# Window attention and a SiLU MLP on one core: the second chunk's maximum sent earlier by GpSimd's queue, block 2's rows shared by two engines, later blocks' steps moved

## The chip, the core and the metric

The kernel runs on one core of a Trainium2 chip. The metric is the device time of one execution in microseconds (us); the median of three runs stands for the kernel. One execution is also profiled. Engines: PE (TensorE), DVE (VectorE), ACT (ScalarE), POOL (GpSimd) and SP (SyncE, which here only issues DMAs). PEld is PE's loading of weights.

## What is computed

The input x has 4 batches of 4096 rows of 192. Each row is replaced by a weighted sum over itself and the six rows before it (zeros ahead of a batch's first), with weights from a softmax over 7 values for each of 8 heads. An MLP follows, without biases:

```python
w = softmax(weight_gen, axis=-1)                  # B, S, 8 heads, 7 taps
x_unf = the 7 rows ending at s, split by head     # zeros ahead of row 0
out = einsum('bshk,bskhg->bshg', w, x_unf)        # 16384 x 192
h = out @ w_in                                    # 192 x 2048
g = h * sigmoid(h)
result = g @ w_out                                # 2048 x 192
```

## The kernel before

A partition holds 128 consecutive rows of x (32 partitions make a batch), plus a halo of the six rows before them. The work goes in 32 blocks of `TB` = 4 rows per partition, 512 rows a block. Blocks are loaded in chunks: chunk 0 is block 0, chunk 1 block 1, chunk 2 blocks 2 and 3, and from chunk 3 on four blocks each, seven such chunks.

For a chunk, `softmax_steps` (lines 288 to 317) makes the weights: `top`, `sub`, `exp`, `tot`, `rec`, `norm`. From chunk 2 on POOL does `sub` and `norm`, ACT `exp`, DVE the rest. `scale_steps` (line 321) finds the largest absolute value of the chunk's x for a power-of-two scale: DVE reduces the rows (line 332) to one value per partition (`m_x`), which has to reach all partitions. `absmax_to_all` does that by PE, for chunk 0 and the weights; `absmax_by_dma` (line 169) writes the 128 values to DRAM (`d_x`) and reads them back to every partition (`mb_x`), both DMAs on SP's queue, and DVE reduces them (line 184).

For a block, `prep_steps` (line 386) makes seven products of x and weights (`mul`, line 396) and adds them up (`add`, line 402), on POOL for the first `share` taps and on DVE for the others; block 2 has all seven on POOL, later blocks three. `hi` on ACT and `lo` on DVE (lines 371, 374) split the result in two fp16 parts `xs`, a DMA transposes it to `xt` and two more swap its halves to `xu`. Blocks 0 and 1 (`early_prep`, line 419) have their products on DVE and the sums on PE in fp32 (line 439).

The MLP goes by pairs of 128 columns of w_in, eight pairs to a block. `mm1` (line 479) makes `h` in PSUM from `xt` and `xu`, 18 matmuls a pair; `act` on ACT makes silu and its fp16 high part `gh` (lines 487, 488); `lower` on DVE makes the low part `gl` (line 493) and with it frees the PSUM tile, of which there are four; `mm2` (lines 507, 516) adds the pair's part of the second product. `finish` (lines 535, 536) scales a block out. `mm1` runs 2 to 4 pairs ahead of `mm2` (`lead_of`): three in the first five pairs of a block, two in the last three.

The fp32 weights w_in and w_out come as integer words and are converted by DVE and ACT in the course of blocks 0 and 1: `merge` (lines 232, 233), then `move`, `shift`, `upper`, `lower` for each pair (lines 242 to 252).

Each engine works off its own list in order, so what matters is where an instruction stands in its engine's list and what it waits for. Two tables set that. `OPENING` gives, for the sixteen pairs of blocks 0 and 1, the steps emitted ahead of a pair's `mm1` and behind its `act`: `m0` to `m6` and `t0` to `t6` are block 1's products and sums, `a` and `b` the reduction of chunk 1's x and its two DMAs, `c` and `d` the reduction of what comes back and the scales, `g` the `gl` of the pair before, `I`, `O`, `i`, `o` the conversion, `x` the maximum of w_out. `START` gives for the steps of later chunks and blocks the half pair at which they are emitted: a time u is worked off behind the half pair of that number, a block has 16 of them, and the times of block b's steps (`any_p` on POOL, `any_v` on DVE) and of a chunk's (`any_s` softmax, `any_x` scale) count from two blocks ahead of it. A step of time 9 stands behind the fifth pair, pair 4; one of time 16 between the two halves of the next block's first pair.

## Time and profile before

| | us |
|---|---|
| median of 3 runs (lowest, highest) | 1115.7 (1114.89, 1116.55) |
| profiled execution, its own time | 1114.89 |
| its span, first to last instruction | 1113.1 |
| PE busy (share of the span) | 1056.1 (95%) |
| DVE, ACT, POOL busy | 800.0, 775.1, 323.6 |

Busy time by stretch of the span, in us:

| stretch | PE | DVE | ACT | POOL | granted PE clock (1 is 2.4 GHz) |
|---|---|---|---|---|---|
| 0 to 60 | 38.68 | 42.65 | 15.45 | 5.22 | 0.78 |
| 60 to 100 | 32.52 | 34.35 | 25.67 | 16.21 | 0.86 |
| 100 to 145 | 36.44 | 35.07 | 28.73 | 17.75 | 0.92 |
| 145 to 1113.1 | 948.46 | 687.97 | 705.20 | 284.45 | 1.00 |

The first three stretches are the opening: blocks 0 and 1 with the conversion of the weights. In a timeline row the brackets at the end give the idle time of the engine just before the instruction and what ended it; a row with x2 or more merges neighbours of one kind. A matmul's end is modelled, so rows of PE overlap.

### The profile page before, as it was taken

The page shows a single profiled execution, that of the slowest core. Times are in us where ns is not written, and L with a number is a line of the kernel's source. Part 1 is how long each engine was busy: PE and PEld are TensorE (multiplying, and loading weights), DVE is VectorE, ACT ScalarE, POOL GpSimd, SP SyncE. Part 2 cuts the span into 40 slices and gives each one's busy share as a digit, 9 for nine tenths or more (in the row PEclk, how much of TensorE's full clock was granted, in tenths as well). Part 3 has the DMA queues.
Part 4 walks back from the last instruction along what each step waited for, and adds up shares of the span by engine and source line. Part 5 has one row for each costly group of instructions (what it writes and reads, how often), then busy time and mean ns, then how long its engine had stood idle before and what let it go on. Part 6 is the DMA issues. An engine that isn't in the chain of part 4 may idle for free.

```text
span 1113.1 us, 37056 instructions
## 1 busy us (share of the span) xinstructions
PE 1056.1 (95%) x16592; PEld 806.7 (72%) x16592; DVE 800.0 (72%) x1158; ACT 775.1 (70%) x1245; POOL 323.6 (29%) x185
## 2 busy tenths in 40 slices
PE   6687999999999999999999999999999999999997
PEld 4344667777777777787777777777777777777776
DVE  6788788666876678666886668766886668766643
ACT  1364787776777777667877777678777768777774
POOL 1008304333252124333061233333043332521100
PEclk8778999999999999999999999999999999999999
DMA  9312104221141113311141111421041112211110
GB/s 244 115 29 98 30 29 142 45 44 31 44 141 30 31 45 93 83 40 44 31 129 42 44 45 31 141 45 37 24 141 45 45 30 45 44 34 31 44 45 16
DMA packets 71453, 68.17 MB, mean 61 GB/s; under 512 B 52607, under 2 KB 64383, under 8 KB 69886
## 3 DMA queue, kind: packets, MB, share of 16 engines
q1 hardware_dynamic: 70592, 63.34, 20.8%
q10 hardware_dynamic: 702, 2.47, 0.9%
q8 instruction: 129, 2.11, 0.8%
q14 instruction: 30, 0.25, 0.1%
HBM read 28.44 MB, written 12.59 MB: 37 GB/s over the span
## 4 chain that ended last, share of the span: by engine, by line
PE 70%; ACT 11%; DVE 10%; issue 4%; DMA 3%; POOL 1%; ACTq 0%; DVEq 0%; POOLq 0%
PE acc L507 35%; PE h L479 34%; ACT h L487 4%; DVE gl L493 3%; ACT gh L488 2%; POOL wc L314 1%; PE acc L516 1%; ACT t L535 1%; ACT L302 1%; DMA raw<-in_moe_w_in_dram 1%; ACT L487 1%; DMA d_x<-m_x 1%; ACT xs L371 1%; ACT wc L302 1%; DVE pr L396 1%
## 5 line engine op out<-in xcount | busy, mean ns | idle before, releaser
L493 DVE SCALAR_TENSOR_TENSOR gl<-h,gup,gh 128x512 f16<-128x512 f32 x512 | 380.3, 746 | 262.7 <-ACT gh L488 262.5
L507 PE MATMUL acc<-wo,gh 64*128 64x192 f16 x7616 | 527.4, 243 | 0.0
L507 PE MATMUL acc<-wo,gl 64*128 64x192 f16 x3808 | 509.6, 243 | 4.5 <-DVE gl L493 4.5
L487 ACT ACTIVATE h<-h,inv 128x512 f32<-128x512 f32 x512 | 336.3, 657 | 250.4 <-PE h L479 248.6
L507 PEld LDWEIGHTS <-gh 64*128 64x128 f16 x7616 | 450.7, 94 | 22.1
L479 PEld LDWEIGHTS <-w 64*128 64x128 f16 x4608 | 284.1, 95 | 232.1 <-issue 35.8
L488 ACT ACTIVATE gh<-h,gup 128x512 f16<-128x512 f32 x512 | 352.0, 688 | 16.7
L479 PE MATMUL h<-xt,w 64*128 64x512 f16 x2304 | 325.3, 380 | 27.2 <-DVE gl L493 17.6
L479 PE MATMUL h<-xu,w 64*128 64x512 f16 x2304 | 321.7, 380 | 0.0
L507 PEld LDWEIGHTS <-gl 64*128 64x128 f16 x3808 | 280.6, 94 | 6.1 <-DVE gl L493 6.1
L396 POOL TENSOR_TENSOR pr<-xc,wc 128x768 f32<-128x768 f32 x94 | 156.1, 1674 | 403.5 <-DVE pr L402 381.3
L402 POOL TENSOR_TENSOR pr<-pr,pr 128x768 f32<-128x768 f32 x64 | 138.1, 2157 | 5.0
L396 DVE TENSOR_TENSOR pr<-xc,wc 128x768 f32<-128x768 f32 x116 | 124.4, 1073 | 9.5 <-POOL wc L314 9.5
L402 DVE TENSOR_TENSOR pr<-pr,pr 128x768 f32<-128x768 f32 x116 | 110.0, 949 | 0.0
L298 POOL TENSOR_TENSOR wc<-wc,wm 128x896 f32<-128x896 f32 (+1 forms) x8 | 13.3, 1658 | 152.3 <-DVE wm L295 152.3
L314 POOL TENSOR_TENSOR wc<-wc,ws 128x896 f32<-128x896 f32 (+1 forms) x8 | 13.3, 1658 | 145.2 <-DVE ws L311 116.3
L536 DVE SCALAR_TENSOR_TENSOR o<-acc,od,t 128x192 f32<-128x192 f32 x120 | 41.6, 407 | 3.3 <-ACT t L535 3.3
L516 PE MATMUL acc<-wo,gh 128*128 128x192 f16 x288 | 39.4, 252 | 4.3 <-ACT wo L249 2.0
L535 ACT ACTIVATE t<-acc,od 128x192 f32<-128x192 f32 x120 | 40.7, 426 | 3.6 <-PE acc L516 3.6
L332 DVE TENSOR_REDUCE xm<-xc 128x1 f32<-128x960 f32 (+4 forms) x32 | 40.9, 1278 | 0.0
L516 PE MATMUL acc<-wo,gl 128*128 128x192 f16 x144 | 36.2, 251 | 2.8 <-DVE gl L493 2.7
L374 DVE SCALAR_TENSOR_TENSOR xs<-pr,xup,xs 128x768 f16<-128x768 f32 x30 | 33.2, 1107 | 2.1
(98 smaller groups left out, 293.8 us busy)
## 6 DMA issues: line engine op xcount, KB each, us to landing
xc<-in_x_dram SPq DMA_DIRECT2D x7, 2112.0 KB, 12.1
xu<-xt SPq DMA_DIRECT2D x62, 192.0 KB, 2.9
out_dram<-o SPq DMA_DIRECT2D x58, 192.0 KB, 1.9
wc<-in_weight_gen_dram SPq DMA_DIRECT2D x7, 448.0 KB, 6.6
rawo<-in_moe_w_out_dram SPq DMA_DIRECT2D x2, 1536.0 KB, 22.0
...
```

Of the source, the lines that this page charges most:

```text
L332: nc.vector.tensor_reduce(out=m[:, i + (c == 1):i + 1 + (c == 1)], in_=x_t[c][:, cuts[i]:cuts[i + 1], :].rearrange("p t d -> p (t d)"), op ...
L374: nc.vector.scalar_tensor_tensor(out=xs[:, ts, D:2 * D], in0=acc, scalar=sc[c, "up"], in1=xs[:, ts, 0:D], op0=ALU.mult, op1=ALU.subtract)
L396: eng.tensor_tensor(out=pr[k].rearrange("p t (h g) -> p (t h) g", g=G), in0=xin, in1=wv, op=ALU.mult)
L402: eng.tensor_tensor(out=pr[k], in0=pr[k], in1=pr[l], op=ALU.add)
L479: nc.tensor.matmul(h_t[b, p + NP * i], w16[rows, g, part, p * P:(p + 1) * P], x_in[rows, :, k, :], start=n == 0, stop=n == NT9 - 1)
L487: nc.scalar.activation(out=h, in_=h, func=AF.Silu, scale=sc[c, "inv"])
L488: nc.scalar.activation(out=gh, in_=h, func=AF.Copy, scale=sc[c, "gup"])
L493: nc.vector.scalar_tensor_tensor(out=gl_t[b, f], in0=h, scalar=sc[chunk_of[b], "gup"], in1=gh_t[b, f], op0=ALU.mult, op1=ALU.subtract)
L507: nc.tensor.matmul(acc_t[b, i, t // 2][:, t % 2, :], g[rows, t * P:(t + 1) * P], wo16[rows, f, part], start=f == ORDER[0] and t % 2 == 0 a ...
L516: nc.tensor.matmul(acc_t[b, 0, t // 2][:, t % 2, :], g[:, t * P:(t + 1) * P], wo16[:, f, part], start=b < 2 and f == 0 and t % 2 == 0 and ...
L535: nc.scalar.activation(out=t1, in_=a[0], func=AF.Copy, scale=sc[c, "od"])
L536: nc.vector.scalar_tensor_tensor(out=o[:, t, :], in0=a[1], scalar=sc[c, "od"], in1=t1, op0=ALU.mult, op1=ALU.add)
```

## The change

The maximum of chunk 1's x is taken between the second and the third maximum of w_in (`parts1[0]()`, `rows1()` ahead of `in_max(2)`) instead of behind the first pair's conversion, and its two DMAs go by GpSimd's queue. Three of the four memsets of halo rows stand behind the first softmax chain. Block 2 has four taps on POOL and three on DVE. The tables are changed to match; in the later chunks the softmax's `tot`, `rec`, `norm` go from 11 to 9, the first reduction of x from -0.5 to 1, the second from 2.5 to 5, the third product on DVE (`any_v`, fourth entry) from 16 to 19.

```diff
-    ("00", "i1u i1l a b m0", "m1 m2"),
+    ("00", "i1u i1l m0 m1", "m2"),
...
-    "c2x": (10.5, 11.5, 11.5, 22.25, 22.25, 22.25),
-    "b2p": (9.9,) * 13,
...
+    "b2p": (12.5,) * 7,
+    "b2v": (16.5, 18.5, 18.5, 20.5, 20.5, 24.5, 24.5, 26.5, 26.5),
+    "any_s": (3, 3, 7, 9, 9, 9),
+    "any_x": (1, 5, 6.5, 9, 9.5, 19.75, 19.75, 20.5),
...
-    def absmax_by_dma(m, name):
+    def absmax_by_dma(m, name, queue=nc.sync):
...
-            nc.sync.dma_start(out=d.unsqueeze(1), in_=m1)
-            nc.sync.dma_start(out=mb, in_=d.partition_broadcast(P))
+            queue.dma_start(out=d.unsqueeze(1), in_=m1)
+            queue.dma_start(out=mb, in_=d.partition_broadcast(P))
...
-            for q in range(0, P, PB):
-                (nc.vector if q == PB else nc.gpsimd).memset(t[q:q + 1, 0:HALO, :], 0.0)
+            nc.gpsimd.memset(t[0:1, 0:HALO, :], 0.0)
+
+            def zeros(queue, q):
+                queue.memset(t[q:q + 1, 0:HALO, :], 0.0)
+            step["zeros"] = zeros
...
         load_in(1, nc.scalar)
+        zeros = step.pop("zeros")
         for f in (tot0, rec0, norm0):
             f()
+        for q, eng in ((PB, nc.vector), (2 * PB, nc.gpsimd), (3 * PB, nc.gpsimd)):
+            zeros(eng, q)
...
+        parts1, (rows1, over1, small1) = scale_steps(1, lambda m, name: absmax_by_dma(m, name, nc.gpsimd))
+        parts1[0]()
+        rows1()
         in_max(2)
...
-                pool, steps, last = prep_steps(b, K if b == 2 else 3)
+                pool, steps, last = prep_steps(b, 4 if b == 2 else 3)
```

Below, lines of the changed kernel are three higher than before from the halo's memsets on.

DVE at the start of the program, before (`xc` x of chunk 0, `wc` the weights of chunks 0 and 1, `wm` and `ws` their maxima and sums):

```order
L272 MEMSET xc_122 1x1152
L295 TENSOR_REDUCE wm_189<-wc_109 128x32
L298 TENSOR_TENSOR wc_109<-wc_109,wm_189 128x224
L295 TENSOR_REDUCE wm_193<-wc_111 128x32
L298 TENSOR_TENSOR wc_111<-wc_111,wm_193 128x224
L306 TENSOR_REDUCE ws_200<-wc_109 128x32
L310 TENSOR_SCALAR ws_200<-ws_200 128x32
L311 RECIPROCAL ws_200<-ws_200 128x32
L314 TENSOR_TENSOR wc_109<-wc_109,ws_200 128x224
L306 TENSOR_REDUCE ws_214<-wc_111 128x32
L310 TENSOR_SCALAR ws_214<-ws_214 128x32
```

and in the changed kernel:

```order
L298 TENSOR_REDUCE wm_186<-wc_109 128x32
L301 TENSOR_TENSOR wc_109<-wc_109,wm_186 128x224
L298 TENSOR_REDUCE wm_190<-wc_111 128x32
L301 TENSOR_TENSOR wc_111<-wc_111,wm_190 128x224
L309 TENSOR_REDUCE ws_197<-wc_109 128x32
L313 TENSOR_SCALAR ws_197<-ws_197 128x32
L314 RECIPROCAL ws_197<-ws_197 128x32
L317 TENSOR_TENSOR wc_109<-wc_109,ws_197 128x224
L274 MEMSET xc_122 1x1152
L309 TENSOR_REDUCE ws_214<-wc_111 128x32
L313 TENSOR_SCALAR ws_214<-ws_214 128x32
```

The memset stands behind the first chunk's norm instead of ahead of both chains.

POOL behind its last memset, where chunk 2's softmax and block 2's products stand, before (`xc_385`, `wc_383` chunk 2; `pr` products):

```order
L298 TENSOR_TENSOR wc_383<-wc_383,wm_449 128x448
L314 TENSOR_TENSOR wc_383<-wc_383,ws_718 128x448
L396 TENSOR_TENSOR pr_0_723<-xc_385,wc_383 128x768
L396 TENSOR_TENSOR pr_1_724<-xc_385,wc_383 128x768
L402 TENSOR_TENSOR pr_0_723<-pr_0_723,pr_1_724 128x768
L396 TENSOR_TENSOR pr_2_725<-xc_385,wc_383 128x768
L402 TENSOR_TENSOR pr_0_723<-pr_0_723,pr_2_725 128x768
L396 TENSOR_TENSOR pr_3_726<-xc_385,wc_383 128x768
L402 TENSOR_TENSOR pr_0_723<-pr_0_723,pr_3_726 128x768
L396 TENSOR_TENSOR pr_4_727<-xc_385,wc_383 128x768
L402 TENSOR_TENSOR pr_0_723<-pr_0_723,pr_4_727 128x768
L396 TENSOR_TENSOR pr_5_728<-xc_385,wc_383 128x768
```

and in the changed kernel, where `pr_0_864` is already block 3:

```order
L178 DMA d_x_262<-m_x_260 128x1
L179 DMA mb_x_263<-d_x_262 128x128
L301 TENSOR_TENSOR wc_383<-wc_383,wm_449 128x448
L317 TENSOR_TENSOR wc_383<-wc_383,ws_718 128x448
L399 TENSOR_TENSOR pr_0_723<-xc_385,wc_383 128x768
L399 TENSOR_TENSOR pr_1_724<-xc_385,wc_383 128x768
L405 TENSOR_TENSOR pr_0_723<-pr_0_723,pr_1_724 128x768
L399 TENSOR_TENSOR pr_2_725<-xc_385,wc_383 128x768
L405 TENSOR_TENSOR pr_0_723<-pr_0_723,pr_2_725 128x768
L399 TENSOR_TENSOR pr_3_726<-xc_385,wc_383 128x768
L405 TENSOR_TENSOR pr_0_723<-pr_0_723,pr_3_726 128x768
L399 TENSOR_TENSOR pr_0_864<-xc_385,wc_383 128x768
```

The two DMAs (`d_x`, `mb_x`) now stand ahead of POOL's work on chunk 2, and block 2 has seven steps where it had thirteen (of which the rows of before show ten).

DVE in a later chunk, behind pair 4 of a block (`gl_4`, `gl_12` are that pair's; `xs` is `lo`, `ws` the softmax sum, `xm` the reduction of x), before:

```order
L493 SCALAR_TENSOR_TENSOR gl_4_7166<-h_4_7145,gup_4985,gh_4_7165 128x512
L493 SCALAR_TENSOR_TENSOR gl_12_7171<-h_12_7146,gup_4985,gh_12_7170 128x512
L374 SCALAR_TENSOR_TENSOR xs_6127<-pr_3_6123,xup_4974,xs_6127 128x4x192
L175 TENSOR_REDUCE m_x_7182<-xm_6873 128x1
L493 SCALAR_TENSOR_TENSOR gl_5_7257<-h_5_7236,gup_4985,gh_5_7256 128x512
L493 SCALAR_TENSOR_TENSOR gl_13_7262<-h_13_7237,gup_4985,gh_13_7261 128x512
L306 TENSOR_REDUCE ws_7266<-wc_4848 128x128
L310 TENSOR_SCALAR ws_7266<-ws_7266 128x128
L311 RECIPROCAL ws_7266<-ws_7266 128x128
L493 SCALAR_TENSOR_TENSOR gl_6_7340<-h_6_7319,gup_4985,gh_6_7339 128x512
L396 TENSOR_TENSOR pr_3_6794<-xc_4850,wc_4848 128x768
L493 SCALAR_TENSOR_TENSOR gl_14_7351<-h_14_7320,gup_4985,gh_14_7350 128x512
```

and in the changed kernel:

```order
L496 SCALAR_TENSOR_TENSOR gl_4_7165<-h_4_7144,gup_4985,gh_4_7164 128x512
L496 SCALAR_TENSOR_TENSOR gl_12_7170<-h_12_7145,gup_4985,gh_12_7169 128x512
L377 SCALAR_TENSOR_TENSOR xs_6127<-pr_3_6123,xup_4974,xs_6127 128x4x192
L309 TENSOR_REDUCE ws_7181<-wc_4847 128x128
L313 TENSOR_SCALAR ws_7181<-ws_7181 128x128
L314 RECIPROCAL ws_7181<-ws_7181 128x128
L335 TENSOR_REDUCE xm_6873<-xc_4849 128x1
L496 SCALAR_TENSOR_TENSOR gl_5_7256<-h_5_7235,gup_4985,gh_5_7255 128x512
L175 TENSOR_REDUCE m_x_7260<-xm_6873 128x1
L496 SCALAR_TENSOR_TENSOR gl_13_7267<-h_13_7236,gup_4985,gh_13_7266 128x512
L496 SCALAR_TENSOR_TENSOR gl_6_7340<-h_6_7319,gup_4985,gh_6_7339 128x512
L399 TENSOR_TENSOR pr_3_6794<-xc_4849,wc_4847 128x768
```

The softmax sum and its reciprocal stood behind pair 5 and the last reduction ahead of pair 4; now all three stand behind `lo`, ahead of pair 5.

## Rows read from the trace of the kernel before

**Rows 1.** Waits of PE from 150 us on: us in total, times, longest.

```profile
PE h L479 <- DVE gl L493: 8.9, 14, 0.7
PE acc L507 <- DVE gl L493: 4.5, 7, 0.7
```

**Rows 2.** Timeline of DVE, 0 to 20: start, us, engine, line, operation.

```profile
7.56 1.02 DVE L272 MEMSET xc<- 1x1152 f32 x1 [6.56 <-DMA xc<-in_x_dram]
...
11.39 0.38 DVE L306 TENSOR_REDUCE ws<-wc 128x32 f32<-128x224 f32 x1
...
12.71 2.14 DVE L332 TENSOR_REDUCE xm<-xc 128x1 f32<-128x1920 f32 x1
...
19.41 1.22 DVE L585 TENSOR_REDUCE wm_in<-raw 128x1 f32<-128x1024 f32 x1 [1.14 <-DMA raw<-in_moe_w_in_dram]
```

**Rows 3.** Timeline of all engines, 16 to 56.

```profile
16.67 10.98 PE L439 MATMUL sum<-pr,ident 128*128 128x384 f32 x28
...
32.62 2.31 PE L479 MATMUL h<-xt,w 64*128 64x512 f16 x9 [1.53 <-ACT w L249]
...
34.31 2.34 PE L479 MATMUL h<-xu,w 64*128 64x512 f16 x9
...
35.38 0.95 DVE L332 TENSOR_REDUCE xm<-xc 128x1 f32<-128x768 f32 x1
...
36.55 0.34 SPq L178 DMA_DIRECT2D d_x<-m_x  x1
...
38.84 9.30 PE L439 MATMUL sum<-pr,ident 128*128 128x384 f32 x28
...
50.39 0.29 DVE L184 TENSOR_REDUCE ra_x<-mb_x 128x1 f32<-128x128 f32 x1 [6.47 <-DMA mb_x<-d_x]
...
55.53 1.03 PE L479 MATMUL h<-xt,w 64*128 64x512 f16 x4 [7.39 <-ACT w L249]
```

**Rows 4.** Busy by stretch: us, PE, PEld, DVE, ACT, POOL, clock, DMA share, GB/s.

```profile
30.00:32.00 2.00, 0.72 (x5) 0.45 (x5) 1.37 (x3) 1.39 (x3) 0.00 (x0) 0.58 0.47 157
```

**Rows 5.** Busy by stretch, as rows 4, around block 2's rows.

```profile
97.60:101.40 3.80, 0.00 (x0) 0.00 (x0) 3.75 (x3) 0.00 (x0) 3.72 (x3) 1.00 0.01 3
105.20:109.40 4.20, 4.20 (x24) 1.89 (x21) 4.17 (x3) 1.09 (x2) 3.35 (x2) 0.57 0.81 342
109.40:128.00 18.60, 16.31 (x159) 11.99 (x158) 12.87 (x29) 14.19 (x24) 0.00 (x0) 1.00 0.01 2
122.05:123.85 1.80, 1.80 (x21) 1.35 (x18) 1.73 (x5) 0.28 (x1) 0.00 (x0) 1.00 0.00 0
```

**Rows 6.** Timeline, 90 to 106: POOL's seventh step, PE's tenth pair.

```profile
95.46 1.81 POOL L402 TENSOR_TENSOR pr<-pr,pr 128x768 f32<-128x768 f32 x1
...
103.91 2.55 PE L479 MATMUL h<-xt,w 64*128 64x512 f16 x9 [6.46 <-DVE gl L493]
```

**Rows 7.** Page, costliest groups: products on DVE, busy, mean ns, idle before.

```profile
L396 DVE TENSOR_TENSOR pr<-xc,wc 128x768 f32<-128x768 f32 x116 | 124.4, 1073 | 9.5 <-POOL wc L314 9.5
```

**Rows 8.** Timeline, 134 to 143: products of block 3, PE's wait.

```profile
135.69 4.77 DVE L396 TENSOR_TENSOR pr<-xc,wc 128x768 f32<-128x768 f32 x2
...
141.18 0.26 PE L516 MATMUL acc<-wo,gl 128*128 128x192 f16 x1 [2.05 <-DVE gl L493]
```

**Rows 9.** Timeline of DVE, 408 to 430, a chunk in the middle.

```profile
410.30 1.34 DVE L332 TENSOR_REDUCE xm<-xc 128x1 f32<-128x1152 f32 x1
...
422.44 1.02 DVE L374 SCALAR_TENSOR_TENSOR xs<-pr,xup,xs 128x768 f16<-128x768 f32 x1
...
425.65 1.08 DVE L306 TENSOR_REDUCE ws<-wc 128x128 f32<-128x896 f32 x1
...
427.89 0.65 DVE L493 SCALAR_TENSOR_TENSOR gl<-h,gup,gh 128x512 f16<-128x512 f32 x1
```

**Rows 10.** Timeline of PE, 424 to 430, the same chunk.

```profile
424.26 0.33 PE L507 MATMUL acc<-wo,gh 64*128 64x192 f16 x2
...
428.22 0.38 PE L479 MATMUL h<-xt,w 64*128 64x512 f16 x1
```

More of the change, by code (lines that the diff above doesn't have):

```diff
@@ L44 @@
     "c2s": (2.75, 4.5, 6, 9.5, 9.5, 9.75),
-    "c2x": (10.5, 11.5, 11.5, 22.25, 22.25, 22.25),
-    "b2p": (9.9,) * 13,
-    "b2v": (25, 25.25, 25.25),
-    "any_s": (2, 3, 7, 11, 11, 11),
-    "any_x": (-0.5, 2.5, 4.5, 6.5, 9, 19.75, 19.75, 20.5),
+    "c2x": (10.5, 11.5, 11.5, 18.25, 18.25, 18.25),
+    "b2p": (12.5,) * 7,
+    "b2v": (16.5, 18.5, 18.5, 20.5, 20.5, 24.5, 24.5, 26.5, 26.5),
+    "any_s": (3, 3, 7, 9, 9, 9),
+    "any_x": (1, 5, 6.5, 9, 9.5, 19.75, 19.75, 20.5),
     "any_p": (11.25,) * 5,
-    "any_v": (12, 13, 15, 16, 20, 20.75, 21.5, 22.25, 24.5, 25, 25),
-    "prep": (9.9, 15),
+    "any_v": (12, 13, 15, 19, 20, 20.75, 21.5, 22.25, 24.5, 25, 25),
+    "prep": (9.9,),
     "chunk2": (2.5,),
@@ L254, in convert_steps @@
         return [move_, shift, upper, lower]
-    x_t, w_t, sc = {}, {}, {}
+    x_t, w_t, sc, step = {}, {}, {}, {}
     def load_x(c):
@@ L674, in lead_of @@
             return 4 if v < 2 else 3 if v < len(OPENING) - 3 or v % NP < 5 else 2
-        parts1, (rows1, over1, small1) = scale_steps(1, absmax_by_dma)
-        step = {"a": parts1[0], "b": rows1, "c": over1, "d": small1, "e": lambda: finish_scales(1),
+        step |= {"c": over1, "d": small1, "e": lambda: finish_scales(1),
                 "f": lambda: out_scale(1), "R": rows_o, "T": turn_o, "V": over_o, "S": spread_o,
```

## The prediction

> **What bounds the kernel now.** I read the busy shares by stretch first (the table above): from 145 us on TensorE (PE) works all but 2% of the time, before that it is idle for 37 us of 145. So the profile has two parts: an opening held up by chains of short steps, and a long PE-bound rest in which only PE's own waits can be won. For the rest I read PE's waits: 14 waits of up to 0.7 us at the first layer's matmuls and 7 of 0.65 us at the second layer's, 13.4 us in all, every one on VectorE's (DVE's) `gl` [rows 1]. They recur in each chunk of four blocks, about 128 us. For the opening I read the timeline engine by engine and asked at each gap which step ended last.
>
> **The opening up to the third pair.** DVE's first real instruction is the memset of a halo row, which waits until 7.56 for the halo's DMA and lasts 1.02; both softmax chains queue behind it. The last four steps of the second chain run from 11.39 to 12.71, where the reduction of x begins [rows 2]. After the change the chains go ahead of the memset. The chunk's weights are the first DMA on both queues, ahead of x and its halo, and the six steps of the first chain with two of the second took 11.39 - 8.58 = 2.8, so I take them to end before 7.56. Then memset (7.56 to 8.58) and 1.32 for the rest: the reduction starts at 9.9, **2.8 us earlier**. The fp32 sums on PE hang on it, run back to back for 10.98 [rows 3] and so end 2.8 earlier too, at 24.9.
>
> The second chunk's reduction and its row maximum (0.95 and about 0.15, 35.38 to 36.5 [rows 3]) now stand before the third maximum of w_in, so they cost 1.1 on DVE at a place where PE waits for DVE next. But DVE also had 1.14 of idle time before the first w_in maximum, for a DMA [rows 2]. That load stands behind the exponentials in ScalarE's (ACT's) queue, which run earlier now. If its data keep ahead, DVE gains 2.8 + 1.14 - 1.1 = 2.8, level with PE. If they land no earlier than now, the gain of 2.8 turns into a loss of 1.1. I take 2.8, since the issue moves by more than 4 us, and keep the rest for the range.
>
> The first pair's matmuls could so start at 32.62 - 2.8 = 29.8. Their second half reads `xu`, swapped by a DMA on SP's queue behind the load of w_out, and the DMA engines are full until about 31 (share 0.47 in 30 to 32 [rows 4]). The bytes are the same, so this end does not move. `xu` was used at 34.31; it can come between 31.6 and 34.3. I take 32.8, about the middle: the second half and all after it on PE gains 1.5, and the sums of block 1, now 38.84 to 48.14 [rows 3], end at 46.6.
>
> DVE then comes to step `c`, where it now idles 6.47 until 50.39 because the maximum's two DMAs, issued from 36.55 on, take 13.84 together [rows 3]. In the change `c` is reached at 43.92 - 2.8 = 41.1 and the maximum is ready at 36.5 - 2.8 - 11.2 = 22.5 (the step stands some 11 us further ahead in DVE's list): a window of **18.6 us**. A DMA on GpSimd's (POOL's) queue is in no row. From below: 13.84, as on SP. (The Trainium skill, DMA: Bandwidth & Descriptors, section "Anatomy of one DMA — SWDGE (gpsimd) path", gives about 2.0 us fixed for one DMA from GpSimd's queue. By it the pair would take some 4 us, an estimate, and the sum would be the same, no wait; the 13.84 that two such small DMAs took on SP [rows 3] speaks against so little, and no run here shows it.) From above: the first DMA gets nothing until the engines are free at 31, then 13.84, which ends at 44.9, 3.8 late. I take about 16, nearer the lower end, because these are the same few bytes: no wait. On POOL only the softmax of chunk 2 is queued behind them, whose input comes after `c`. On SP the loads of chunk 2 lose the two DMAs ahead of them and leave earlier.
>
> With the 6.47 gone the third pair's weights are ready at 55.53 - 6.47 - 2.8 = 46.3, and PE is free at 46.6. So it starts at 46.65 where it started at 55.53 [rows 3]: **gain 8.9**. What follows to 75 us is the DVE and ACT conversion of the weights in the same order, and shifts by that.
>
> **Block 2's rows.** POOL makes block 2's seven products and six sums until 108.6 (3.35 busy from 105.2 on [rows 5]), and DVE's integer steps beside it are slow: merging one piece of w_out takes 1.73 alone and 3.75 for half a piece beside POOL; the piece of w_in, of the same size, takes 4.17 [rows 5]. PE waits 6.46 for it, until 103.91 [rows 6]. With four products POOL ends with what is now its seventh step, at 95.46 + 1.81 = 97.3 [rows 6]. The first half of the merge stays slow, the second falls from 3.75 to 0.9, and the step behind it saves some 0.5 (an estimate at the same ratio): PE resumes at 100.5, 3.4 earlier. The w_in merge saves 4.17 - 1.73 = 2.4 and DVE's first product of block 2 costs 1.0 (mean 1.07 of such a product [rows 7]). Against this stand DVE's other two products and three sums, some 5 us over the next four pairs. From 109.4 to 128 DVE is idle 18.60 - 12.87 = 5.7 and PE 2.3 [rows 5], so they fill time that is free: I charge nothing, and from PE's own waits there take 0.5 as gained with the shorter merges. Sum: 3.4 + 2.4 - 1.0 + 0.5 = **5.3**; bounds 0.3 (the 5 us all in PE's way) and 6.
>
> At 135.69 two products of block 3 take 4.77 on DVE because POOL makes its share beside them, and PE waits 2.05 [rows 8]. POOL's share waits for the tile that DVE's conversion of block 2 frees; after the change a sum one pair earlier frees it, so POOL starts sooner by more than a pair and is nearly done by then: **2.3** gained, with the small wait behind it. Bounds: 0 to 2.3.
>
> **The later chunks.** Three waits per chunk go. At the first pair of a block the reduction of x and a product stood between its two `gl`; both move behind it. In the seventh pair a product waited 9.5 / 7 = 1.36 for POOL's norm [rows 7]; the norm moves two pairs up. At the next first pair a product slowed by POOL moves to the second pair. That is 13.4 in all. But the change packs three things behind pair 4: `lo` (1.0 from 422.44), the softmax sum with its reciprocal (2.24, 425.65 to 427.89) and the last reduction (1.3, as at 410.30) [rows 9]. Run by hand on the chunk at 400 us, 0.70 earlier throughout: DVE takes `lo` at 421.74 as ACT allows, is through at 426.3 and, 0.75 later, has the first `gl` of pair 5 at 427.0. PE asks for it in the second of the two second-layer groups between 424.26 and 428.22 [rows 10], that is at 426.23 - 0.70 + 0.15 = 425.7, and waits 1.3; the other `gl` of the pair, 0.75 behind the first, costs 0.5 more. So a **new wait of 1.8 per chunk**, 12.6 in seven, takes the place of 13.4: net 0.8. Bounds: the packed steps fit somewhere that I don't see (13.4 gained), or one of them is slowed by POOL's norm beside it (3 per chunk, 8 lost).
>
> **Sum.** 8.9 + 5.3 + 2.3 + 0.8 = 17.3. The profiled execution has 1114.89 (span 1113.1), which gives 1097.6; the median of the runs is 0.8 higher: **1098**. No change means within 0.2%, 2.2 us, which is about what a measurement of this kernel can tell.
>
> **The rivals.**
> *The new wait does not come.* For it: the chunk's steps are the same work in another order, and PE has groups of 4 us per pair in hand before pair 5. Against it: 4.5 us of DVE steps stand between two `gl` where now at most 2.3 do [rows 9]. Then another 12.6 go: 1085.5. Chance 0.18.
> *GpSimd's DMAs come late, but come.* The wait of 6.47 shrinks instead of going, or xu or w_in land late in the opening. In the rows DVE and POOL shut each other out: 1.73 against 4.17 [rows 5]. The Trainium skill (SBUF — State Buffer, section "SBUF: two separate sides") makes a mechanism of this: GpSimd's cores write the descriptors of a DMA issued from their queue, and cannot while DVE holds the shared port, so such a DMA can stand still beside DVE work. No run here shows it yet, and by that rule alone both DMAs would wait for a DVE step or two, not for many. With 3 to 7 us lost of the opening: 1101 to 1105, and 1103 in the middle. Chance 0.14.
> *Slower.* The same DMA pair starves for good: GpSimd is kept from its port by DVE, which is busy 42.65 of the first 60 us. DVE stands at `c` all that time, and with it the weights of all later pairs, one us per us. The gains elsewhere are 17.3, so it decides from 18.6 + 17.3 = 36 us for the pair on; at 45 us the kernel takes 1125. For it: no row prices that queue. Against it: it would be three times the 13.84 of SP's. Chance 0.06.
> *The change does nothing here*, if the opening's gain is eaten at PE's start by w_in landing late and the new wait is 3 us: 1114. Chance 0.05.
>
> **How the numbers follow.** My case, 1098 with 1092 to 1103 from its bounds, has 0.57. The range goes down to the first rival and up past the second: 1084 to 1107. It leaves out the last two and the tails of the first. Faster by over 0.2%: 0.57 + 0.18 + 0.14 = 0.89; within: 0.04; slower: 0.07 (the third rival and a little of the fourth).
>
> **What would show it.** Right: DVE's x reduction at about 9.9, no wait of DVE at `c`, the third pair's matmuls near 46.7, POOL's block 2 with 7 steps and PE's wait before the tenth pair near 3 instead of 6.46, and from there one PE wait of 1 to 2 us per chunk on `gl` of pair 5 instead of three of 0.6 to 0.7. Wrong: a wait of DVE on `mb_x` at `c`; a wait of the third w_in maximum on its DMA at 22 to 25 us; no wait at pair 5, or one of over 2.5 us.

## The result, and the profile after

The changed kernel takes 1100.71 us (median of 3 runs, 1100.29 to 1100.84) against 1115.7: ratio 0.9865, 95% interval 0.9842 to 0.9887. The forecast was 1098 with 1084 to 1107, and 1092 to 1103 for its own case. The time lies inside both, but the terms did not come out one by one. The profiled execution of after has 1100.84, its span 1099.0, 14.1 less than before.

| | before | after |
|---|---|---|
| DVE, ACT, POOL busy, us | 800.0, 775.1, 323.6 | 810.7, 774.6, 309.0 |
| PE busy 0 to 60, 60 to 100, 100 to 145 | 38.68, 32.52, 36.44 | 39.68, 32.58, 43.58 |
| granted PE clock there | 0.78, 0.86, 0.92 | 0.80, 0.93, 0.99 |

The lead of after over before, read at the same point of the program:

| point | before | after | lead | forecast |
|---|---|---|---|---|
| third pair's matmuls | 55.53 | 52.66 | 2.9 | 8.9 |
| ninth pair's matmuls | 92.96 | 88.83 | 4.1 | 8.9 |
| first store behind 100 us | 144.22 | 133.56 | 10.7 | 16.5 |
| end of the span | 1113.1 | 1099.0 | 14.1 | 17.3 |

So the opening up to the ninth pair gave 4.1 instead of 8.9, the rows of blocks 2 and 3 gave 6.5 instead of 7.6, and the later chunks 3.4 instead of 0.8. That the time still lies between 1092 and 1103 owes something to luck: over half of the 4.8 that the opening lacks is made up by 2.6 that the later chunks gave beyond their forecast.

**The opening.** Timeline of the changed kernel, DVE, 0 to 20 (columns as in the timelines above):

```profile
10.36 2.15 DVE L335 TENSOR_REDUCE xm<-xc 128x1 f32<-128x1920 f32 x1
...
17.14 1.22 DVE L588 TENSOR_REDUCE wm_in<-raw 128x1 f32<-128x1024 f32 x1 [1.22 <-DMA raw<-in_moe_w_in_dram]
```

The reduction of x starts at 10.36 where it started at 12.71 [rows 2]; 9.9 was forecast. In experiments 1, 3, 4, 6, 8, 10 and 11, with the same code up to there, it starts at 9.63 to 9.92. That step held. The next did not: the wait before the first maximum of w_in, counted as gained, is still there (1.22, before 1.14 [rows 2]), since its data landed only 2.3 earlier, though ACT issued its loads of w_in at 4.90 instead of 10.18. With the 1.1 of the second chunk's reduction to pay, the first pair starts at 31.41, 1.2 earlier than before, and not at 29.8.

Timeline of the changed kernel, all engines, 24 to 56:

```profile
24.32 0.71 POOL L178 DMA_DIRECT2D d_x<-m_x  x1 [14.72 <-DVE m_x L175]
...
31.41 2.31 PE L482 MATMUL h<-xt,w 64*128 64x512 f16 x9 [1.69 <-ACT w L249]
...
35.72 0.56 POOL L179 DMA_DIRECT2D mb_x<-d_x  x1 [10.69 <-DMA xu<-xt]
...
37.71 2.29 PE L482 MATMUL h<-xu,w 64*128 64x512 f16 x9 [4.00 <-DMA xu<-xt]
...
43.43 9.30 PE L442 MATMUL sum<-pr,ident 128*128 128x384 f32 x28
...
45.60 0.28 DVE L184 TENSOR_REDUCE ra_x<-mb_x 128x1 f32<-128x128 f32 x1
...
52.66 1.25 PE L482 MATMUL h<-xt,w 64*128 64x512 f16 x9
```

DVE doesn't wait at `c` any more (45.60, no bracket; before 6.47 [rows 3]). But PE, which had `xu` at 34.31 before, now waits 4.00 for it and goes on at 37.71; 32.8 was forecast. All that follows on PE is late by that, and by another 1.2 because the second pair's matmuls ran at the clock's lower level (granted clock 0.50, which is 1.2 GHz, in 36 to 40 and 0.62 in 40 to 44, before 0.85 and 1.00): from the second half of the first pair to the end of the sums it is 15.0 us, before 13.8. The third pair stands right behind the sums. (POOL's 10.69 ahead of the read back at 35.72 is put down to `xu`; by its landing, 24.32 + 11.1 = 35.4, it is `d_x` that it waited for.) Issue to landing of this `xu` (the tile's view, 20 to 50: least, median and most), before and after, then busy time by stretch around it, before and after (columns as in rows 4):

```profile
DMA to landing us min/median/max: 2.2/2.4/2.6
```

```profile
DMA to landing us min/median/max: 7.2/7.3/7.6
```

```profile
30.00:34.00 4.00, 2.09 (x13) 1.02 (x15) 2.73 (x7) 2.29 (x5) 0.00 (x0) 0.54 0.61 177
```

```profile
30.00:34.00 4.00, 2.31 (x9) 0.59 (x9) 2.79 (x12) 1.60 (x3) 0.00 (x0) 0.50 0.43 65
```

`xu` took 7.3 where it took 2.4 before, at a time when the DMA engines moved 65 GB/s instead of 177. That was in no step of the prediction, and experiments 1 to 3 and 5 go after it.

From the third pair to the ninth 1.2 more came in: 0.9 up to the fifth pair, 1.4 from there to the sixth, and 1.0 was lost again by the ninth, where PE now waits 0.56 for `gl`. Between the fifth pair and the sixth PE has the same 67 or 68 matmuls, before and after:

```profile
70.47:80.55 10.08, 7.75 (x67) 5.98 (x68) 8.53 (x19) 9.25 (x14) 0.00 (x0) 0.83 0.00 1
```

```profile
66.75:75.43 8.68, 6.34 (x68) 4.80 (x68) 7.56 (x17) 8.47 (x13) 0.00 (x0) 1.00 0.00 1
```

Before, 10.08 at a granted clock of 0.83; after, 8.68 at 1.00. In stretches of 4 us the granted clock was 0.50 to 0.51 from 52 to 68 before, behind 7.39 of idle time; after, where the third pair follows the sums, it was 1.00 from 44 to 60, 0.57 from 60 to 64, behind 4 us in which PE worked 1.08, and 1.00 again up to 80. No term of mine had this.

**Block 2's rows.** Timeline of the changed kernel, POOL and DVE, then PE:

```profile
91.68 1.81 POOL L405 TENSOR_TENSOR pr<-pr,pr 128x768 f32<-128x768 f32 x1
...
91.86 2.04 DVE L233 SCALAR_TENSOR_TENSOR rawo<-rawo 128x384 int32<-128x384 int32 x1
...
94.21 0.56 DVE L233 SCALAR_TENSOR_TENSOR rawo<-rawo 128x384 int32<-128x384 int32 x1
...
96.74 0.37 PE L482 MATMUL h<-xt,w 64*128 64x512 f16 x1 [3.06 <-DVE gl L496]
```

POOL's seventh step is its last and ends at 93.5. DVE's merge beside it still takes 2.04, the same merge behind it 0.56. PE's wait before the tenth pair is 3.06, where it was 6.46 [rows 6] and "near 3" was forecast.

**The later chunks.** PE's waits from 150 on (us in all, times, longest), and a chunk in the middle on PE, DVE and POOL:

```profile
PE h L482 <- DVE gl L496: 5.3, 13, 0.6
PE acc L510 <- DVE gl L496: 2.1, 7, 0.3
```

```profile
397.20 0.75 DVE L496 SCALAR_TENSOR_TENSOR gl<-h,gup,gh 128x512 f16<-128x512 f32 x1 [0.15 <-ACT gh L491]
...
399.89 1.76 POOL L301 TENSOR_TENSOR wc<-wc,wm 128x896 f32<-128x896 f32 x1 [17.33 <-DVE wm L298]
...
400.38 2.08 DVE L405 TENSOR_TENSOR pr<-pr,pr 128x768 f32<-128x768 f32 x1
...
402.16 0.38 PE L482 MATMUL h<-xt,w 64*128 64x512 f16 x1
...
403.18 1.04 PE L482 MATMUL h<-xt,w 64*128 64x512 f16 x8 [0.64 <-DVE gl L496]
...
404.04 1.24 PE L482 MATMUL h<-xu,w 64*128 64x512 f16 x9
...
407.49 1.04 PE L482 MATMUL h<-xt,w 64*128 64x512 f16 x8 [0.21 <-DVE gl L496]
...
416.49 0.26 PE L510 MATMUL acc<-wo,gl 64*128 64x192 f16 x2 [0.30 <-DVE gl L496]
...
421.63 0.75 DVE L496 SCALAR_TENSOR_TENSOR gl<-h,gup,gh 128x512 f16<-128x512 f32 x1 [1.23 <-ACT gh L491]
```

The three waits of 0.6 to 0.7 per chunk [rows 1] have become 0.64 and 0.21 at two pairs one behind the other early in the block, and 0.30 with a smaller one at pair 5. The forecast had one of 1.8, at pair 5. DVE shows why there are three: from 397.20 to 420.40 it is never idle, and a sum in that stretch takes 2.08, with POOL's `sub`, now right behind `top`, beside it; another such sum, at 405.83 with POOL idle, takes 0.94.

### The profile page after: what moved, and what is told of

Same layout as the page of the kernel before. It is cut to its first block, busy times and chain, and to the rows that moved or that the text cites. A ratio compares the mean times of both kernels' runs of the same rounds, so it can differ in the third digit from the quotient of the medians.

```text
span 1099.0 us, 37055 instructions
## 1 busy us (share of the span) xinstructions
PE 1054.7 (96%) x16592; PEld 762.2 (69%) x16592; DVE 810.7 (74%) x1164; ACT 774.6 (70%) x1245; POOL 309.0 (28%) x181
## 3 DMA queue, kind: packets, MB, share of 16 engines
HBM read 28.44 MB, written 12.59 MB: 37 GB/s over the span
## 4 chain that ended last, share of the span: by engine, by line
PE 73%; DVE 16%; ACT 5%; issue 3%; DMA 2%; DVEq 0%; ACTq 0%
PE h L482 36%; PE acc L510 36%; DVE gl L496 4%; DVE xm L335 3%; DVE pr L405 2%; ACT h L490 2%; ACT gh L491 2%; DVE pr L399 1%; DMA raw<-in_moe_w_in_dram 1%; PE sum L442 1%; DVE xs L377 1%; DVE ws L309 1%; DMA xu<-xt 1%; DVE wm L298 1%; PE acc L519 1%
## 5 line engine op out<-in xcount | busy, mean ns | idle before, releaser
L510 PE MATMUL acc<-wo,gh 64*128 64x192 f16 x7616 | 493.9, 243 | 0.0
L510 PE MATMUL acc<-wo,gl 64*128 64x192 f16 x3808 | 473.7, 243 | 2.9 <-DVE gl L496 2.1
L482 PEld LDWEIGHTS <-w 64*128 64x128 f16 x4608 | 234.1, 95 | 241.2 <-issue 26.8
L510 PEld LDWEIGHTS <-gh 64*128 64x128 f16 x7616 | 362.3, 94 | 45.2
L482 PE MATMUL h<-xt,w 64*128 64x512 f16 x2304 | 324.6, 380 | 13.3 <-DVE gl L496 10.7
L399 POOL TENSOR_TENSOR pr<-xc,wc 128x768 f32<-128x768 f32 x91 | 145.7, 1615 | 426.7 <-DVE pr L405 426.0
L510 PEld LDWEIGHTS <-gl 64*128 64x128 f16 x3808 | 200.1, 94 | 6.1 <-DVE gl L496 6.1
L405 POOL TENSOR_TENSOR pr<-pr,pr 128x768 f32<-128x768 f32 x61 | 132.5, 2172 | 4.8
L405 DVE TENSOR_TENSOR pr<-pr,pr 128x768 f32<-128x768 f32 x119 | 120.9, 1016 | 0.1
L377 DVE SCALAR_TENSOR_TENSOR xs<-pr,xup,xs 128x768 f16<-128x768 f32 x30 | 39.2, 1308 | 1.6
L519 PE MATMUL acc<-wo,gl 128*128 128x192 f16 x144 | 35.5, 246 | 1.3 <-DVE gl L496 1.1
```

The source lines that it names most:

```text
L377: nc.vector.scalar_tensor_tensor(out=xs[:, ts, D:2 * D], in0=acc, scalar=sc[c, "up"], in1=xs[:, ts, 0:D], op0=ALU.mult, op1=ALU.subtract)
L399: eng.tensor_tensor(out=pr[k].rearrange("p t (h g) -> p (t h) g", g=G), in0=xin, in1=wv, op=ALU.mult)
L405: eng.tensor_tensor(out=pr[k], in0=pr[k], in1=pr[l], op=ALU.add)
L482: nc.tensor.matmul(h_t[b, p + NP * i], w16[rows, g, part, p * P:(p + 1) * P], x_in[rows, :, k, :], start=n == 0, stop=n == NT9 - 1)
L510: nc.tensor.matmul(acc_t[b, i, t // 2][:, t % 2, :], g[rows, t * P:(t + 1) * P], wo16[rows, f, part], start=f == ORDER[0] and t % 2 == 0 a ...
L519: nc.tensor.matmul(acc_t[b, 0, t // 2][:, t % 2, :], g[:, t * P:(t + 1) * P], wo16[:, f, part], start=b < 2 and f == 0 and t % 2 == 0 and ...
```

## The experiments

Times are medians of 4 or 5 runs, beside runs of the kernel before on the same chip. Experiments 1 to 8, 10 and 11 are the changed kernel (1100.71) with the one edit named; 9 and 12 join several. For the late `xu` there were two theories: chunk 2's loads, which now leave right behind it (A), and the write of `d_x`, which now is in flight beside it (B).

**1. Chunk 2's loads behind xu.** In the changed kernel they leave SP's queue 1.2 us behind `xu`, since SP no longer stands at the maximum's DMAs.

```diff
-    def load_x(c):
+    def load_x(c, queue=nc.sync):
...
-                load_w(c)
-                load_x(c)
+                load_w(c, nc.scalar if c == 2 else nc.sync)
+                load_x(c, nc.scalar if c == 2 else nc.sync)
```

> The changed kernel with the two loads of chunk 2 (wc and xc, 448 of 896... the first of them 224 KB, the second 1344 KB) on ACT's queue, behind pair 0's activations, which themselves wait for xu; in the changed kernel they leave on SP's queue 1.2 us behind xu. Theory A (these loads take the DMA engines' turns from xu): xu lands 2 to 3 us after its issue instead of 7.3, PE's wait of 4.0 on xu goes, the third pair starts at 48.5 to 49.5 instead of 52.66, and the kernel takes about 1097. Theory B (the 0.5 KB write of d_x to DRAM, issued at 24.32 and landed at 35.4, holds up whatever the DMA engines carry meanwhile): xu still takes 6 to 7.5, PE still waits 3 to 4 for it, and the time stays within 2 us of 1100.7.

Measured: 1100.28 (1099.61 to 1101.83). `xu` still takes 7.2 to 7.8, and PE waits 4.30:

```profile
37.97 2.29 PE L482 MATMUL h<-xu,w 64*128 64x512 f16 x9 [4.30 <-DMA xu<-xt]
```

```profile
30.00:34.00 4.00, 2.31 (x9) 0.58 (x9) 2.95 (x12) 1.60 (x3) 0.00 (x0) 0.50 0.49 73
```

73 GB/s in 30 to 34, with the loads gone from there. Theory A falls: `xu` is as slow without the loads behind it.

**2. The maximum's DMAs late.** Reduction and both DMAs back behind the first pair's conversion, still on POOL's queue.

```diff
-    ("00", "i1u i1l m0 m1", "m2"),
+    ("00", "i1u i1l a b m0 m1", "m2"),
...
-        parts1[0]()
-        rows1()
...
-        step |= {"c": over1, "d": small1, "e": lambda: finish_scales(1),
+        step |= {"a": parts1[0], "b": rows1, "c": over1, "d": small1, "e": lambda: finish_scales(1),
```

> The changed kernel with the reduction of chunk 1's x and the issue of its two DMAs back in their old place behind the first pair's conversion (DVE at about 34), still on GpSimd's queue; chunk 2's loads still leave on SP right behind xu. Theory A: xu still takes 6 to 7.5 us to land and PE waits about 3 to 4 for it, and on top DVE waits at c for the maximum; 1103 to 1108. Theory B: xu lands 2 to 3 us after its issue, no PE wait on xu, the second half of the first pair at about 32.5 to 33.5; d_x is then written from about 34 on and lands 7 to 11 later, and DVE waits 4 to 9 at c; the third pair at 51 to 55 and the kernel at 1099 to 1103.

Measured: 1100.88 (1099.96 to 1101.54).

```profile
33.51 2.29 PE L482 MATMUL h<-xu,w 64*128 64x512 f16 x9 [0.89 <-DMA xu<-xt]
...
45.85 0.28 DVE L184 TENSOR_REDUCE ra_x<-mb_x 128x1 f32<-128x128 f32 x1 [4.25 <-DMA mb_x<-d_x]
...
50.98 1.66 PE L482 MATMUL h<-xt,w 64*128 64x512 f16 x9 [2.74 <-ACT w L249]
```

```profile
30.00:34.00 4.00, 2.80 (x13) 0.90 (x15) 3.58 (x12) 0.79 (x2) 0.00 (x0) 0.50 0.96 265
34.00:36.00 2.00, 2.00 (x12) 0.74 (x10) 1.97 (x5) 0.56 (x1) 0.71 (x1) 0.50 0.99 392
```

The same loads stand behind `xu`, but no `d_x` is in flight: 265 GB/s, `xu` lands after 4.1, PE waits 0.89. That is Theory B, but for the 4.1 (2 to 3 were expected; what costs `xu` the rest isn't shown). One thing speaks against the theory as it is worded: here `d_x` is issued at 34.51 and lands 7.3 later, and the loads still move 392 GB/s from 34 to 36. A write that is merely in flight doesn't hold up whatever the DMA engines carry. DVE now waits 4.25 at `c`. The third pair starts 1.7 earlier than in the changed kernel, and the time is the same within the runs' spread: early DMAs and a late `xu`, or late DMAs and an early `xu`, are worth the same here.

**3. The early DMAs on SP's queue.**

```diff
-        parts1, (rows1, over1, small1) = scale_steps(1, lambda m, name: absmax_by_dma(m, name, nc.gpsimd))
+        parts1, (rows1, over1, small1) = scale_steps(1, lambda m, name: absmax_by_dma(m, name, nc.sync))
```

> The changed kernel with chunk 1's maximum in its new place, but its two DMAs on SP's queue, as before the change. There the read back stands ahead of SP's half of xu and waits for the write. Theory A: the write lands about 7.5 us after its issue at 24.3, so at 32; SP's xu is issued at about 32.5 and lands at 35 with the loads of chunk 2 behind it; the first pair's second half at 35 to 36, 2 us earlier than in the changed kernel; about 1099. Theory B: the write lands at 35 as on GpSimd's queue and SP's xu only after it, at 38 to 42; the first pair's second half 1 to 5 us later than at 37.71; 1101 to 1106.

Measured: 1103.89 (1103.08 to 1105.34), as Theory B has it. Issue to landing of `d_x` and `mb_x` (the tile's view: least, median, most) in the changed kernel and here, and PE here:

```profile
DMA to landing us min/median/max: 6.8/9.0/11.1
```

```profile
DMA to landing us min/median/max: 4.9/8.2/11.5
```

```profile
35.54 0.61 PE L482 MATMUL h<-xu,w 64*128 64x512 f16 x1 [2.34 <-DMA xu<-xt]
...
41.18 1.89 PE L482 MATMUL h<-xu,w 64*128 64x512 f16 x8 [5.04 <-DMA xu<-xt]
```

```profile
30.00:34.00 4.00, 2.31 (x9) 0.59 (x9) 2.99 (x12) 1.38 (x3) 0.00 (x0) 0.50 0.21 49
```

The write of `d_x` takes 11.1 on POOL's queue and 11.5 on SP's. So it isn't the queue that makes it slow; what POOL's queue wins is that SP's half of `xu` isn't held behind it: 3.2 us. (The 49 GB/s are no measure of the write here, since SP's queue itself stands behind the read back until 35.5.) The Trainium skill (SBUF — State Buffer, section "SBUF: two separate sides") has a DMA from GpSimd's queue stand still while a DVE operation holds the port that the two share; with DVE as busy in both, 11.1 against 11.5 shows nothing of it here.

**4. The old times of the later blocks.**

```diff
-    "any_s": (3, 3, 7, 9, 9, 9),
-    "any_x": (1, 5, 6.5, 9, 9.5, 19.75, 19.75, 20.5),
-    "any_v": (12, 13, 15, 19, 20, 20.75, 21.5, 22.25, 24.5, 25, 25),
+    "any_s": (2, 3, 7, 11, 11, 11),
+    "any_x": (-0.5, 2.5, 4.5, 6.5, 9, 19.75, 19.75, 20.5),
+    "any_v": (12, 13, 15, 16, 20, 20.75, 21.5, 22.25, 24.5, 25, 25),
```

> The changed kernel with the old times of the later blocks (softmax, scale and the fourth entry of DVE's products). The prediction gave the new times a net gain of 0.8: the kernel would take 1101.5. By the stores of the two traces, where the lead grows from 11.2 behind block 2 to 14.1 at the end, they are worth 2.9: 1103.6. In both the PE waits of before come back: 14 of 0.6 to 0.7 at the first layer's matmuls and 7 of 0.65 at the second's.

Measured: 1104.21 (1104.11 to 1105.26). The new times are worth 3.5, not 0.8.

**5. Chunk 1's maximum by PE, no write to DRAM.** A transpose and a product with ones, in PSUM tiles that are free then; the reduction stays in its new place.

```diff
...
-        parts1, (rows1, over1, small1) = scale_steps(1, lambda m, name: absmax_by_dma(m, name, nc.gpsimd))
+        parts1, (rows1, turn_x1, over1, spread1, small1) = scale_steps(1, lambda m, name: absmax_to_all(m, name, ps_o))
...
-        start = [rows, turn, hi0, hi1, lambda: merge_in(0), over, spread, lo0, scales_in, move_a, lo1,
+        start = [rows, turn, turn_x1, hi0, hi1, lambda: merge_in(0), over, spread, lo0, scales_in, move_a, lo1,
...
-                 lambda: turn_x(1, nc.vector.tensor_copy), lower_a, lambda: step.pop("i1s")(),
+                 lambda: turn_x(1, nc.vector.tensor_copy), over1, spread1, lower_a, lambda: step.pop("i1s")(),
...
```

> The changed kernel with chunk 1's maximum brought to all partitions by PE (a transpose and a product with ones, as for chunk 0, through two free PSUM tiles) in place of the two DMAs, so that no d_x is written to DRAM in the opening; chunk 2's loads stay right behind xu on SP. Theory B (the small DRAM write in flight holds up the other DMAs): no drop of the bytes moved to under 100 GB/s between 30 and 35; xu lands 2.4 to 4.5 us after its issue, PE's wait of 4.0 on xu shrinks to at most 1, the third pair starts at 47.5 to 49.5 instead of 52.66 and the kernel takes 1096 to 1098.5. If it isn't the write (a rival: xu is slow because of something else that lies at 29 to 37 us): xu still takes 7, the third pair stays at 52 to 53, 1100 to 1101.

Measured: 1096.86 (1096.61 to 1097.88), 3.85 less than the changed kernel.

```profile
DMA to landing us min/median/max: 2.6/3.1/4.5
```

```profile
30.00:34.00 4.00, 2.85 (x11) 1.14 (x12) 3.23 (x12) 1.14 (x3) 0.00 (x0) 0.50 0.86 242
```

```profile
34.29 2.29 PE L484 MATMUL h<-xu,w 64*128 64x512 f16 x9 [1.33 <-DMA xu<-xt]
...
48.68 1.25 PE L484 MATMUL h<-xt,w 64*128 64x512 f16 x9
```

Without the write, 242 GB/s in the same stretch, `xu` after 3.1, and the third pair at 48.68. PE still waits 1.33 for `xu`, against "at most 1"; in experiments 9 and 12, with the same opening, it doesn't wait at all. So it is the early write that makes `xu` late, in every trace: with the write at 24 on POOL's queue (after, 1, 4, 6, 8, 10, 11) `xu` takes 6.5 to 8.2 and 65 to 105 GB/s move from 30 to 34; with it late or gone (2, 5, 9, 12) `xu` takes 2.6 to 4.5 and 192 to 265 move. But the write does nothing visible before 30. Changed kernel, 24 to 30, with `d_x` issued at 24.32 and not landed:

```profile
24.00:30.00 6.00, 3.89 (x23) 1.95 (x21) 5.63 (x15) 2.48 (x4) 0.71 (x1) 0.95 1.48 366
```

Before, with no write there, it was 359.

**6. Block 2's products all on POOL again** (share, `b2p`, `b2v` and `c2x` as before).

```diff
...
-                pool, steps, last = prep_steps(b, 4 if b == 2 else 3)
+                pool, steps, last = prep_steps(b, K if b == 2 else 3)
```

> The changed kernel with block 2's rows as before: all seven products on POOL, thirteen steps, DVE only the parts hi and lo, old times. The prediction gave the sharing 5.3: 1106.0. In the two traces the lead grows from 3.5 at the first matmul of the eighth pair after the opening's gap to 9.3 at the start of the block behind: 5 to 6. PE's wait before the tenth pair would be 5.5 to 7 again instead of 3.06, and DVE's merges 3.5 to 4.2 instead of 0.9 and 1.65. A rival: the wait was that long only because of what went before it, and 2 us come back at most.

Measured: 1108.95 (1106.68 to 1109.83): the sharing is worth 8.2, with runs 3 us apart. PE's two waits of before are back, those before the tenth pair and in block 3 [rows 6, 8]:

```profile
100.45 2.55 PE L482 MATMUL h<-xt,w 64*128 64x512 f16 x9 [6.44 <-DVE gl L496]
...
136.50 0.26 PE L519 MATMUL acc<-wo,gl 128*128 128x192 f16 x1 [2.04 <-DVE gl L496]
```

So block 3's 2.3 belongs to this part, as the prediction had it; its two terms make 7.6.

**7. The halo memsets ahead of the chains.**

```diff
+        for q, eng in ((PB, nc.vector), (2 * PB, nc.gpsimd), (3 * PB, nc.gpsimd)):
+            zeros(eng, q)
         for f in (top0, sub0, exp0, top1, sub1, exp1):
```

> The changed kernel with the three halo memsets ahead of the softmax chains again. Prediction's step: the x reduction starts 2.4 to 2.8 later, and everything up to the first pair with it; 1102.5 to 1103.5. Rival: the opening's end is set by xu, which the write of d_x holds up; the write moves with DVE, so xu lands 2 us later as well, but if it is the end of the w_out load that sets xu, nothing changes: 1100.5 to 1101.

Measured: 1101.29 (1101.16 to 1101.35). The x reduction starts at 12.59 again, 2.2 later, and the end is 0.6 later, between the two expectations: while `xu` is held up (PE waits 3.30 for it here, 4.00 in the changed kernel), the first chain has slack.

**8. Three steps of the later blocks moved again.** The first reduction of x to a place where DVE idles, `top` and `sub` away from DVE's sum, the last reduction behind pair 5.

```diff
-    "any_s": (3, 3, 7, 9, 9, 9),
-    "any_x": (1, 5, 6.5, 9, 9.5, 19.75, 19.75, 20.5),
+    "any_s": (1, 1, 7, 9, 9, 9),
+    "any_x": (-1, 5, 6.5, 10.5, 11, 19.75, 19.75, 20.5),
...
-            at(START["chunk2"][0] if c == 2 else u0, prepare)
+            at(START["chunk2"][0] if c == 2 else u0 - 1, prepare)
```

> The changed kernel with three of the later blocks' steps moved again: the first reduction of x from behind the second half pair to the last half pair of the block before, where DVE idles 1.0 us, the softmax maximum (and POOL's sub) from 3 to 1, so that POOL's sub doesn't run beside DVE's sum, the last reduction from 9 to 10.5 (and the row maximum to 11). In the changed kernel PE waits some 1.35 us per chunk at three places. If those waits are DVE's queue of steps as in the trace, 4 to 8 of the 9 us in seven chunks go: 1093 to 1097. If the steps only move the wait (to pair 1's gl, or DVE waiting for the maximum's read back at the next block), the time stays within 2 us of 1100.7.

Measured: 1088.67 (1087.89 to 1090.55), 12.0 less, more than was expected and more than the 7.4 us (5.3 and 2.1) that the changed kernel's trace lists from 150 on for PE's waits on `gl`. Here, from 150 on, PE waits for no `gl` of the first layer; the stores one chunk apart give the period (before, after, here):

```profile
407.45 0.99 SPq L539 DMA_DIRECT2D out_dram<-o  x2
...
535.64 0.99 SPq L539 DMA_DIRECT2D out_dram<-o  x2
```

```profile
395.76 0.99 SPq L542 DMA_DIRECT2D out_dram<-o  x2
...
523.45 0.99 SPq L542 DMA_DIRECT2D out_dram<-o  x2
```

```profile
392.58 0.99 SPq L542 DMA_DIRECT2D out_dram<-o  x2
...
518.44 0.99 SPq L542 DMA_DIRECT2D out_dram<-o  x2
```

128.19, 127.69 and 125.86 us per chunk. Measured against 125.86, the best that a version shows, before loses 2.33 per chunk and after 1.83.

**9. Experiments 5 and 8 together.**

> The maximum by PE and the moved steps of the later blocks together. The one lies before 55 us and the other behind 150: if they add up, 1100.7 - 3.85 - 12.0 = 1084.8, 1084 to 1086. If the earlier opening is eaten by a wait further on, 1086 to 1089.

Measured: 1085.33 (1083.81 to 1088.03), ratio to before 0.9731 (0.9717 to 0.9746). They add up; no other version has a lower median. PE doesn't wait for `xu` and comes to its half at 33.32 (34.31 before, 37.71 in the changed kernel, 32.8 forecast), and the third pair starts where the prediction put it (46.65):

```profile
33.32 2.29 PE L484 MATMUL h<-xu,w 64*128 64x512 f16 x9
...
46.91 1.25 PE L484 MATMUL h<-xt,w 64*128 64x512 f16 x9
```

**10. Of experiment 8, the last reduction alone.**

```diff
-    "any_x": (1, 5, 6.5, 9, 9.5, 19.75, 19.75, 20.5),
+    "any_x": (1, 5, 6.5, 10.5, 11, 19.75, 19.75, 20.5),
```

> The changed kernel with only the last reduction of x and the row maximum moved (9 to 10.5 and 9.5 to 11), which the prediction counted among the three things packed behind pair 4. By the prediction this packing costs 1.8 us per chunk, of which the reduction's 1.3 would come back: some 9 us, 1091 to 1093. By the trace of the changed kernel, where pair 5's two waits are 0.2 and 0.30, it costs some 0.5 per chunk: 3 to 4 us, 1096.5 to 1098.

Measured: 1093.46 (1093.19 to 1094.19), 7.25 less. The prediction's 9 is nearer than the 3 to 4 of the listed waits.

**11. Of experiment 8, the first reduction, `top` and `sub` alone.**

```diff
-    "any_s": (3, 3, 7, 9, 9, 9),
-    "any_x": (1, 5, 6.5, 9, 9.5, 19.75, 19.75, 20.5),
+    "any_s": (1, 1, 7, 9, 9, 9),
+    "any_x": (-1, 5, 6.5, 9, 9.5, 19.75, 19.75, 20.5),
...
-            at(START["chunk2"][0] if c == 2 else u0, prepare)
+            at(START["chunk2"][0] if c == 2 else u0 - 1, prepare)
```

> The changed kernel with only the first reduction of x (1 to -1) and the softmax maximum with POOL's sub (3 to 1) moved. By the prediction nothing was left to win there, since no new wait was seen in the first pairs: 1100 to 1101, pair 5's wait staying. By the trace (waits of 0.64 and 0.21 per chunk at the block's second and third pair, behind a sum that POOL's sub slows to 2.08) most of the 12 us of the three moves lies here: 1091 to 1095.

Measured: 1097.21 (1096.35 to 1098.07), 3.5 less; both expectations miss. PE's waits from 150 on:

```profile
PE acc L510 <- DVE m_x L175: 6.6, 7, 1.0
```

The first layer's waits are gone and a new one stands at pair 5, 6.6 in seven chunks: PE comes earlier to the reduction that is still packed there. One stretch of DVE's, 23 us long in the changed kernel, sets PE's pace; where the wait shows is only where the two meet. Experiments 10 and 11 make 7.25 + 3.5 of experiment 8's 12.0.

**12. Experiment 9 with three of block 2's taps on POOL.**

```diff
-    "b2p": (12.5,) * 7,
-    "b2v": (16.5, 18.5, 18.5, 20.5, 20.5, 24.5, 24.5, 26.5, 26.5),
+    "b2p": (12.5,) * 5,
+    "b2v": (16.5, 18.5, 18.5, 20.5, 20.5, 22.5, 22.5, 24.5, 24.5, 26.5, 26.5),
...
-                pool, steps, last = prep_steps(b, 4 if b == 2 else 3)
+                pool, steps, last = prep_steps(b, 3)
```

> The maximum by PE, the moved steps, and three of block 2's taps on POOL instead of four. If what is left of PE's wait before the tenth pair (3.07) comes from POOL's last two steps beside DVE's merge of w_out (1.70 and 2.05 for half a piece, against 0.35 and 0.56 for the other half), POOL ends 3.7 earlier, the wait falls to 0.5 or less and the kernel takes 2 to 3 us less than with four taps. If DVE's additional product and sum (1.9) get in PE's way, no gain or a loss of up to 2.

Measured: 1086.51 (1084.02 to 1087.21) against 1085.33 for 9: no difference that these runs show. The wait before the tenth pair goes (1.58 in 9), and one of 1.79 comes at 111.16; in the profiled execution PE also waits 2.4 once, between 700 and 800, for an `xu` (0.8 in 9):

```profile
111.16 0.37 PE L484 MATMUL h<-xt,w 64*128 64x512 f16 x1 [1.79 <-DVE gl L498]
```

## Why the prediction was right, and where its terms were not

- **Memset and reduction: right. The wait for w_in: a term that failed.** The reduction moved 2.35 of the forecast 2.8. The data of w_in moved by 2.3, and to end DVE's wait they had to move by 2.8 + 1.14; so the 1.14 that was counted as gained stayed, and the first pair came 1.2 earlier and not 2.8. In the changed kernel that cost nothing, since PE then waits for `xu`; and in experiment 9, where PE doesn't, the third pair starts at 46.91 behind a first at 31.14. So the whole first chain was worth 0.6 in the changed kernel (experiment 7).
- **xu: the step that failed.** "The bytes are the same, so this end does not move", and `xu` at 32.8. It came at 37.7, 4.9 later. I had bounded it by the end of the w_out load and by the old 34.31, and never asked what the earlier write of `d_x` does to the DMAs around it. Experiments 1, 2, 3 and 5 show that it is the early write, not chunk 2's loads or the queue. Experiment 5 takes back 3.85 us, and with its opening the forecast of this step comes true: `xu` used at 33.32 and 32.73, the third pair at 46.91 and 46.47 (9 and 12).
- **No wait at `c`: right, by a margin that luck made.** I took 16 us for the pair of DMAs and a window of 18.6. The write took 11.1, and the read back, issued at 35.72, 6.8: from 24.32 to 42.5, 18.2 us. `c` came at 45.6 only because `xu` was late; at the 41.1 that I forecast, DVE would have waited 1.4.
- **The opening, 8.9 forecast, 4.1 measured.** At the third pair 6.0 are missing, 4.9 by `xu` and some 1.2 by the clock in the second pair; between the fifth pair and the sixth the clock gave 1.4 back. That PE's clock would differ at the same matmuls was in no step.
- **Block 2's and block 3's rows, 7.6 forecast: 6.5 in the two traces, 8.2 by experiment 6.** Right, with PE's wait at 3.06 as said.
- **The later chunks, 0.8 forecast, 3.5 measured.** The new loss came out in size, 1.8 per chunk and 1.83 against experiment 8, but in part by luck: I charged it all to `lo`, the softmax sum and the last reduction, at pair 5 alone. It shows at three places, and of the 12.0 the last reduction by itself brings 7.25 (experiment 10), while the first reduction, `top` and `sub`, which I charged nothing, bring 3.5 (11). What I mis-sized is the other side: I took the old waits at the 13.4 that the profile lists, and they cost 2.33 per chunk, 16.3 in seven. A listed wait runs from the modelled end of the matmul before. At 402.16 a matmul starts, at 403.18 the next, 1.02 later, where the eight behind it start 0.11 apart (403.18 to 404.04); 0.91 is lost, and 0.64 is listed. That is one reason; whether it is the only one isn't shown.
- **The rivals.** Of "DMAs come late, but come", the half with `xu` late came true, and cost what that rival gave it (3 to 7). That it didn't move the total past 1103 is the later chunks' doing. Starving of GpSimd's DMAs didn't occur. The fourth rival's 1114 doesn't come out of its own terms: without the 8.9, and with 8 lost in place of 0.8 gained, the sum is -0.4, about 1116.

What stays open is how a write of 0.5 KB in pieces of 4 bytes keeps other DMAs waiting, and why only from 30 on, when 366 GB/s moved beside it from 24 to 30; a wider `d_x` was not tried. The Trainium skill (DMA: Bandwidth & Descriptors, section "Back-pressure in remote DMA") says of transfers between cores that "Stalled writes stall the source SDMA engine's other queues too"; these runs, on one core and to DRAM, show a picture like it (65 to 105 GB/s from 30 to 34 with the early write, 192 to 265 with it late or gone), not its cause.
